# Attention on one core: values loaded in pieces of four keys instead of eight

## The chip, the core and the metric

The kernel runs on one core of a Trainium2 chip. The metric is the device time of one execution in microseconds; lower is better. Five engines work side by side and are kept in step by semaphores: TensorE (PE, with its weight loads as PEld) multiplies matrices, VectorE (DVE) and ScalarE (ACT) read its results, GpSimd (POOL) helps with elementwise work, and SyncE (SP) only issues transfers. The transfers themselves run on 16 DMA engines.

## The reference

```python
B, H, Sq, Sk, D = 16, 32, 192, 1024, 128      # all bf16
def reference(q, k, v):
    scale = q.shape[-1] ** -0.5
    scores = jnp.einsum("bhqd,bhkd->bhqk", q, k) * scale
    p = _softmax(scores, axis=-1)
    return jnp.einsum("bhqk,bhkd->bhqd", p, v)
```

There are 512 heads. Each has 192 queries, 1024 keys and 1024 values of 128 numbers. The order in which the 1024 keys are taken is free, as long as keys and values of a head are taken in the same order.

## The kernel before

**Groups, pairs and units.** Heads are handled in 32 groups of 16 (`G`). Within a group, two heads make a pair, with 384 query rows: three units of 128 rows (A from the first head, B from the second, S with 64 rows of each). Two pairs make one turn of the written-out orders `PE_ORDER`, `DVE_ORDER` and `ACT_ORDER`, in which each engine executes its steps; a tick behind a name means the unit of an earlier turn. A group is four turns, 24 units.

**What happens to a unit.** `qk` multiplies 128 queries by all 1024 keys into PSUM (`s_ps`, two matmuls of 512 columns; four for an S unit). VectorE (L333) copies the scaled scores to SBUF and takes the row extreme. For four of six units ScalarE (L374) takes the exponential, for the other two ("shifted") GpSimd only subtracts (L208) and the exponential comes later. `tr` transposes the 1024 columns in eight blocks of 128 on TensorE (L283, into `pt_ps`), ScalarE moves them to SBUF (L383 or L385), and `pv` multiplies each block `t` by the values of the same 128 keys (L317), summing the eight blocks in `o_ps`. VectorE divides by the row sums and writes bf16 to `ob` (L358). All matmuls are issued in the helper `product`, so the profile gives them its line, L221.

**Which keys make a block.** Keys are loaded with a DMA transpose (L148), so that the 128 numbers of a key lie along the partitions. The source is read as rows of eight keys, `(g p) (t d)` with `t` = 8: key `8 p + t` of a head becomes column `p` of block `t`. The values have to follow: partition `p` gets the eight values `8 p` to `8 p + 7`, which are 2048 consecutive bytes of memory (L138 to L141).

**Who issues what, in which order.** SyncE's queue holds, for each group: the keys of the group two ahead (L148), its queries (L152, also a DMA transpose), and the stores of the group's results (L172) in three parts of 80, 44 and 4 partitions (`STORE_PARTS`). Before the keys it waits until the last `qk` of the group that has used the same buffer (`NS` = 2) is done, before the stores until `ob` is full. The first two groups' values are issued by SyncE too. From then on ScalarE issues a group's values, one DMA of 4 MB, after the step `("ev", 15)` of the group before; it first waits until the buffer's last `pv` is done and until that group's keys have landed (L390 to L394). TensorE waits for the queries and the keys at the first `qk` of a group (L258, L267), and for the values at its first `pv` (L314).

Of the kernel before, what the change touches and what calls it, by code (L numbers as in the profile page):

```python
# [5 lines left out]
BF16 = mybir.dt.bfloat16  # L6
# [27 lines left out]
def _attention_kernel(nc, q, k, v, out, G=16, NS=2, NSS=5, NX=4, NPT=5,  # L34
# [10 lines left out]
    KT_TILES = SK // 128  # L45
# [6 lines left out]
    kf = k.rearrange("b h s d -> (b h) s d")  # L52
    vf = v.rearrange("b h s d -> (b h) s d")
# [16 lines left out]
    with ExitStack() as es:  # L70
        def sb(name, shape, dt):
            return es.enter_context(nc.sbuf_tensor(name, shape, dt))
# [4 lines left out]
        def sem(name):  # L77
            return es.enter_context(nc.semaphore(name))

        kt = sb("kt", [128, NS, KT_TILES, G * 128], BF16)  # L80
        qt = sb("qt", [128, NS, G * SQ], BF16)
        vs = sb("vs", [128, NS, G, KT_TILES, 128], BF16)
        ob = sb("ob", [128, NSO, PPG, 3, 128], BF16)
        ss = sb("ss", [128, NSS, SK], F32)
        nb = sb("nb", [128, NSS], F32)
# [28 lines left out]
        def unit_info(u):  # L114
            name = UNITS[u % 6]
            pr = 2 * (u // 6) + int(name[1])
            return pr, "ABS".index(name[0]), pr // PPG, pr % PPG
# [18 lines left out]
        def load_v(e, g, a, b, sm):  # L136
            h0 = g * G
            e.dma_start(  # L138
                vs[:, g % NS, a:b],
                vf[h0 + a:h0 + b].rearrange("g (p t) d -> p g t d", t=KT_TILES),  # L140
            ).then_inc(sm, 16)  # L141

        @block.sync
        def _(e):
            def load_kq(g, a, b, sems):
                s = g % NS
                h0 = g * G
                e.dma_start_transpose(  # L148
                    kt[:, s, :, a * 128:b * 128],
                    kf[h0 + a:h0 + b].rearrange("g (p t) d -> (g p) (t d)", t=KT_TILES),  # L150
                ).then_inc(sems[0], 16)
                e.dma_start_transpose(  # L152
                    qt[:, s, a * SQ:b * SQ],
                    qf[h0 + a:h0 + b].rearrange("g r d -> (g r) d"),
                ).then_inc(sems[1], 16)

            def loads(g):
                s = g % NS
                last_u = (g - NS + 1) * UPG - 1
                if g >= NS:  # L160
                    e.wait_ge(s_qk, last_u + 1)
                load_kq(g, 0, G, (sxk[s], sxq[s]))
                if g < NS:
                    load_v(e, g, 0, G, svl[s])

            def stores(g, a, b):
                so = g % NSO
                e.wait_ge(s_on, g * PPG + b)
                rows = of[g * G + 2 * a:g * G + 2 * b].rearrange("h r d -> (h r) d").rearrange(
                    "(n p) d -> p n d", p=128)  # L170
                for lo, hi in (((0, 128),) if g == NGR - 1 else STORE_PARTS):
                    e.dma_start(  # L172
                        rows[lo:hi],
                        ob[lo:hi, so, a:b].rearrange("p pg y d -> p (pg y) d"),
                    ).then_inc(sst[so], 16)

            n = len(FIRST)
            for i in range(n):
                load_kq(0, *FIRST[i], (sf[i], sf[i]))
                if i > 0:  # L180
                    for i2 in range(i if i > 1 else 0, i + 1):
                        load_v(e, 0, *FIRST[i2], sfv[i2])
            for g in range(1, min(NS, NGR)):
                loads(g)
            for g in range(NGR):
                if g + NS < NGR:
                    loads(g + NS)
                for a, b in (LAST if g == NGR - 1 else ((0, PPG),)):
                    stores(g, a, b)
            for so in range(min(NSO, NGR)):  # L190
                n = len(range(so, NGR - 1, NSO)) * len(STORE_PARTS)
                if so == (NGR - 1) % NSO:
                    n += len(LAST)
                e.wait_ge(sst[so], 16 * n)
# [23 lines left out]
        def _(pe):  # L218
            def product(o, w, x, at=(0, 0), start=True, stop=True, transpose=False):

                return pe.add_instruction(mybir.InstMatmult(  # L221
                    name=nc.get_next_instruction_name(),
                    engine=mybir.EngineType.PE,
                    ins=[pe.lower_ap(x), pe.lower_ap(w)],
                    outs=[pe.lower_ap(o)],
                    start_tensor_calc=start,
                    stop_tensor_calc=stop,
                    is_transpose=transpose or None,
                    tile_size=(128, w.shape[-1]),
                    tile_position=at,  # L230
                    bass_skip_group_check=True,
                    ldweights=False,
                ))
# [4 lines left out]
            def qk(u):  # L238
                pr, k3, g, pg = unit_info(u)
                s = g % NS  # L240
                a = 2 * pg
                b = 2 * pg + 1
                S = s_ps[u % 2]
                if k3 < 2:
                    x0 = a * SQ if k3 == 0 else b * SQ + 64
                    tiles = [((0, 0), slice(0, 128), a if k3 == 0 else b, qt[:, s, x0:x0 + 128])]
                else:
                    tiles = [
                        ((0, 0), slice(0, 64), a, qt[:, s, a * SQ + 128:a * SQ + 192]),
                        ((0, 64), slice(64, 128), b, qt[:, s, b * SQ:b * SQ + 64]),  # L250
                    ]
                if g == 0:
                    for i, (h, _) in enumerate(FIRST):
                        if h <= b and i not in seen_kq:
                            seen_kq.add(i)
                            pe.wait_ge(sf[i], 32)
                elif u % UPG == 0:
                    pe.wait_ge(sxq[s], load_cnt(g))  # L258
                ins = None
                for c in range(2):  # L260
                    cs = slice(4 * c, 4 * c + 4)
                    for at, ps_, x, w in tiles:
                        if c == 0:
                            pe.ldweights(w, tile_position=at)  # L264
                            if at[1] == 0:
                                if g > 0 and u % UPG == 0:
                                    pe.wait_ge(sxk[s], load_cnt(g))  # L267
                                if u >= 2:
                                    pe.wait_ge(s_max, u - 1)
                        ins = product(S[ps_, cs], w, kt[:, s, cs, x * 128:x * 128 + 128], at)  # L270
                ins.then_inc(s_qk, 1)

            def tr(u):
# [12 lines left out]
            def pv(u):  # L286
                pr, k3, g, pg = unit_info(u)
                s = g % NS
                O = o_ps[pr % 2]
                PTS = pt_sb[:, u % NPT]  # L290
                sl = O_SLOT[k3]
                a = 2 * pg
                b = 2 * pg + 1
                ins = None
                with_rs = shifted(u)
                if k3 < 2:
                    tiles = [((0, 0), slice(0, 128), a if k3 == 0 else b)]
                else:
                    tiles = [((0, 0), slice(0, 64), a), ((0, 64), slice(64, 128), b)]
                pe.wait_ge(s_ev, u + 1)  # L300
                for t in range(KT_TILES):
                    first = t == 0
                    last = t == KT_TILES - 1
                    for at, rows, x in tiles:
                        w = PTS[:, t, rows]
                        pe.ldweights(w, tile_position=at)  # L306
                        if first and at[1] == 0:
                            if g == 0:
                                for i, (h, _) in enumerate(FIRST):
                                    if h <= b and i not in seen_v:  # L310
                                        seen_v.add(i)
                                        pe.wait_ge(sfv[i], 16)
                            elif u % UPG == 0:
                                pe.wait_ge(svl[s], load_cnt(g))  # L314
                            if k3 == 0 and pr >= 2:
                                pe.wait_ge(s_on, pr - 1)
                        ins = product(O[rows, sl, :], w, vs[:, s, x, t, :], at, first, last)  # L317
                        if with_rs:
                            ins = product(O[rows, 3, sl: sl + 1], w, ones[:, 0:1], at, False, last)
                ins.then_inc(s_pv, 1)  # L320
# [112 lines left out]
```

## Time and profile before

| what | value |
|---|---|
| time, median of 3 runs | 1200.33 us (1194.54 to 1207.98) |
| the profiled execution's own time | 1195.41 us |
| its span, first to last instruction | 1193.6 us |
| granted TensorE clock | 0.984 |
| HBM read and written | 134.22 MB and 25.17 MB |
| value load of a group (ScalarE's queue), issue to landing, median | 16.3 us |
| key load (SyncE), issue to landing, median | 21.1 us |
| query load (SyncE), issue to landing, median | 8.4 us |

The profile is one execution. Its page gives, in order: the busy time of each engine; the span in 40 slices; the DMA queues with their packets and the time that these took; the chain of work that ended last, followed back from the end; the costliest groups of instructions; and the DMA issues. Queue q1 is SyncE's, q10 is ScalarE's. SPq and ACTq are the issuing queues of SyncE and ScalarE: a DMA instruction there lasts until its queue has taken it, not until the data has landed. In tables of stretches, each row has the stretch, its length, busy time of PE, PEld, DVE, ACT and POOL with the number of instructions, the granted clock, the mean busy share of the 16 DMA engines (over 1 where the times of packets overlap) and what they moved in GB/s.

### The profile page before, as it was taken

Reading aid. Unit: us, or ns where it says so; the run is one execution under the profiler, and the core shown is the slowest. Engines: PE = TensorE matmul, PEld = TensorE weight load, DVE = VectorE, ACT = ScalarE, POOL = GpSimd, SP = SyncE. Lnnn points to the kernel's source line nnn. Section 1 sums busy time; section 2 is a strip of 40 time slices with the busy share of each in tenths; the row PEclk is TensorE's granted clock in tenths of the full one; section 3 lists DMA queues with packets and bytes.
Section 4 is the critical chain, followed back from the end, with each engine's and each line's share of the span. In section 5 each row is a group of like instructions: output and inputs, shape, how many; then the busy total and the mean of one; then the engine's idle time right before and its main releaser. Section 6 shows DMA issues by size and latency. Waiting matters only on the chain.

```text
span 1193.6 us, 38884 instructions
## 1 busy us (share of the span) xinstructions
PE 1127.5 (94%) x18432; PEld 847.8 (71%) x15360; DVE 1088.2 (91%) x2304; ACT 1082.4 (91%) x1793; POOL 485.8 (41%) x262
## 2 busy tenths in 40 slices
PE   5698999999989999999999999999999999999998
PEld 2476767777767777777776777777777777777766
DVE  5587989999989999999998999999999999999987
ACT  4677989999999999999997999999999999999988
POOL 2233434434434434444443444444344344444432
PEclk9888999999999999999998999999999999999999
DMA  9999999999999999999999999999999999999991
GB/s 234 243 282 268 270 248 247 288 297 290 288 256 267 275 304 281 285 276 274 289 283 280 266 251 279 295 303 278 275 265 268 292 284 290 271 271 277 291 245 41
DMA packets 790348, 321.26 MB, mean 269 GB/s; under 512 B 724641, under 2 KB 724641, under 8 KB 790177
## 3 DMA queue, kind: packets, MB, share of 16 engines
q1 hardware_dynamic: 728257, 192.95, 83.9%
q10 hardware_dynamic: 61920, 125.83, 28.9%
q8 instruction: 132, 2.16, 0.7%
q14 instruction: 39, 0.32, 0.1%
HBM read 134.22 MB, written 25.17 MB: 134 GB/s over the span
## 4 chain that ended last, share of the span: by engine, by line
PE 58%; DMA 29%; ACT 7%; SPq 5%; issue 0%; DVE 0%
PE o_ps L221 21%; PE pt_ps L221 19%; DMA vs<-in_v_dram 19%; PE s_ps L221 18%; DMA qt<-in_q_dram 11%; SPq L148 5%; ACT x_sb L374 4%; ACT pt_sb L385 2%; ACT pt_sb L383 1%; SPq L152 0%; SPq L138 0%; DVE ob L358 0%; DVE rinv L356 0%
## 5 line engine op out<-in xcount | busy, mean ns | idle before, releaser
L333 DVE TENSOR_SCALAR_CACHE_REDUCE ss<-s_ps 128x1024 f32<-128x1024 f32 x768 | 920.4, 1220 | 89.1 <-PE s_ps L221 72.8
L208 POOL TENSOR_TENSOR x_sb<-ss,nb 128x1024 bf16<-128x1024 f32 x256 | 485.1, 1895 | 695.9 <-DVE ss L333 665.7
L374 ACT ACTIVATE x_sb<-ss,nb 128x1024 bf16<-128x1024 f32 x512 | 585.4, 1145 | 12.9 <-DVE ss L333 12.9
L306 PEld LDWEIGHTS <-pt_sb 128*128 128x128 bf16 (+1 forms) x8192 | 443.2, 104 | 213.5 <-issue 115.6
L221 PE MATMUL s_ps<-kt,qt 128*128 128x512 bf16 (+1 forms) x2048 | 467.9, 386 | 47.5 <-DMA qt<-in_q_dram 47.0
L221 PE MATMUL o_ps<-vs,pt_sb 128*128 128x128 bf16 (+1 forms) x8192 | 497.5, 219 | 14.2 <-DMA vs<-in_v_dram 13.9
L221 PE MATMUL pt_ps<-ident,x_sb 128*128 128x128 bf16 x6144 | 453.1, 220 | 1.3 <-ACT pt_sb L383 1.3
L280 PEld LDWEIGHTS <-x_sb 128*128 128x128 bf16 x6144 | 367.5, 98 | 62.5 <-issue 62.1
L385 ACT ACTIVATE pt_sb<-pt_ps 128x512 f32<-128x512 f32 x512 | 306.2, 598 | 78.7 <-PE pt_ps L221 77.8
L383 ACT ACTIVATE pt_sb<-pt_ps 128x1024 bf16<-128x1024 bf16 x256 | 260.4, 1017 | 14.4 <-PE pt_ps L221 14.3
L221 PE MATMUL o_ps<-ones,pt_sb 128*128 128x1 bf16 x2048 | 191.2, 166 | 0.0
L358 DVE TENSOR_TENSOR ob<-o_ps,rinv 128x384 bf16<-128x384 f32 x256 | 142.7, 557 | 8.8
L264 PEld LDWEIGHTS <-qt 128*128 128x128 bf16 (+1 forms) x1024 | 79.6, 104 | 66.6 <-DMA qt<-in_q_dram 44.0
L374 ACT ACTIVATION_READ_ACCUMULATOR x_sb<-ss,nb 128x1 f32 x512 | 100.7, 197 | 0.0
L333 DVE DVE_READ_ACCUMULATOR ss<-s_ps 128x1 f32 x768 | 63.8, 83 | 0.0
L356 DVE RECIPROCAL rinv<-o_ps 128x1 f32<-128x1 f32 x256 | 41.8, 163 | 4.2 <-PE o_ps L221 4.2
L346 DVE RECIPROCAL rinv<-rs 128x2 f32<-128x2 f32 x256 | 40.9, 160 | 1.1 <-ACT x_sb L374 1.1
L374 ACT ACT_TABLE_LOAD x1 | 1.3, 1283 | 0.8 <-PEq L418 0.8
L200 POOL TENSOR_SCALAR_AFFINE_SELECT ident<-ones 128x128 bf16<-128x128 bf16 x1 | 0.3, 295 | 0.1
L198 POOL MEMSET ones<- 128x128 bf16 x1 | 0.2, 205 | 0.3 <-POOLq L418 0.3
L418 POOL MEMSET const-float32-0.0<- 128x1 f32 x1 | 0.1, 100 | 0.3 <-issue 0.3
L418 POOL MEMSET const-uint8-127<- 128x1 uint8 x1 | 0.1, 103 | 0.0
(2 smaller groups left out, 0.2 us busy)
## 6 DMA issues: line engine op xcount, KB each, us to landing
vs<-in_v_dram ACTq DMA_DIRECT2D x30, 4096.0 KB, 16.3
out_dram<-ob SPq DMA_DIRECT2D x31, 480.0 KB
out_dram<-ob SPq DMA_DIRECT2D x31, 264.0 KB
vs<-in_v_dram SPq DMA_DIRECT2D x1, 4096.0 KB, 15.1
vs<-in_v_dram SPq DMA_DIRECT2D x1, 2048.0 KB, 9.9
vs<-in_v_dram SPq DMA_DIRECT2D x1, 1536.0 KB, 8.6
out_dram<-ob SPq DMA_DIRECT2D x31, 24.0 KB
kt<-in_k_dram SPq DMA_TRANSPOSE x34, 21.1
```

The source lines that it names most:

```text
L148: e.dma_start_transpose(kt[:, s, :, a * 128:b * 128], kf[h0 + a:h0 + b].rearrange("g (p t) d -> (g p) (t d)", t=KT_TILES),).then_inc(sems[ ...
L208: gp.tensor_tensor(x_sb[:, u % NX, :], ss[:, u % NSS, :], nb[:, u % NSS: u % NSS + 1].to_broadcast([128, SK]), ALU.subtract,).then_inc(s_x ...
L221: return pe.add_instruction(mybir.InstMatmult(name=nc.get_next_instruction_name(), engine=mybir.EngineType.PE, ins=[pe.lower_ap(x), pe.low ...
L264: pe.ldweights(w, tile_position=at)
L280: pe.ldweights(w, is_transpose=True, tile_position=(0, 0))
L306: pe.ldweights(w, tile_position=at)
L333: dve.tensor_scalar(ss[:, u % NSS, :], s_ps[u % 2][:].rearrange("p t k -> p (t k)"), -scale, None, ALU.mult, ALU.min, accum_out=nb[:, u % ...
L356: dve.reciprocal(rinv[:, pr % 2, sel], o_ps[pr % 2][:, 3, sel]).then_inc(s_ri, 1)
L358: dve.tensor_tensor(ob[:, so, pg], o_ps[pr % 2][:, 0:3, :], rinv[:, pr % 2, 0:3].unsqueeze(2).to_broadcast([128, 3, 128]), ALU.mult,).then ...
L374: act.activation(x_sb[:, u % NX, :], ss[:, u % NSS, :], ACT_FN.Exp, bias=nb[:, u % NSS: u % NSS + 1], scale=-1.0, accum_out=rs[:, pr % NRS ...
L383: act.activation(pt_sb[:, u % NPT], pt_ps[u % 2][:], ACT_FN.Exp, scale=-1.0).then_inc(s_ev, 1)
L385: act.activation(words(pt_sb[:, u % NPT]), words(pt_ps[u % 2][:]), ACT_FN.Copy).then_inc(s_ev, 1)
```

## The change

A head's 1024 keys are taken as two halves (`y`) of 512, and a partition gets four consecutive values of each half: key `512 y + 4 p + t`. One DMA still brings a group's values; each of its contiguous pieces has 1024 bytes. The keys are read as rows of four keys, 256 rows a head, so that a transposed block `t` has 256 columns, the first 128 of half 0 and the others of half 1. A score matmul takes two blocks of 256 columns instead of four of 128. In `pv`, step `t` of eight multiplies by half `t % 2`, key `t // 2` of four. Sizes of buffers, waits and orders stay.

```diff
-        kt = sb("kt", [128, NS, KT_TILES, G * 128], BF16)
+        kt = sb("kt", [128, NS, 4, G * 256], BF16)
-        vs = sb("vs", [128, NS, G, KT_TILES, 128], BF16)
+        vs = sb("vs", [128, NS, 2 * G, 4, 128], BF16)
...
         def load_v(e, g, a, b, sm):
             h0 = g * G
             e.dma_start(
-                vs[:, g % NS, a:b],
-                vf[h0 + a:h0 + b].rearrange("g (p t) d -> p g t d", t=KT_TILES),
+                vs[:, g % NS, 2 * a:2 * b],
+                vf[h0 + a:h0 + b].rearrange("g (y p t) d -> p (g y) t d", y=2, t=4),
             ).then_inc(sm, 16)
...
                 e.dma_start_transpose(
-                    kt[:, s, :, a * 128:b * 128],
-                    kf[h0 + a:h0 + b].rearrange("g (p t) d -> (g p) (t d)", t=KT_TILES),
+                    kt[:, s, :, a * 256:b * 256],
+                    kf[h0 + a:h0 + b].rearrange("g (p t) d -> (g p) (t d)", t=4),
                 ).then_inc(sems[0], 16)
...
-                        ins = product(S[ps_, cs], w, kt[:, s, cs, x * 128:x * 128 + 128], at)
+                        ins = product(S[ps_, cs], w, kt[:, s, 2 * c:2 * c + 2, x * 256:x * 256 + 256], at)
...
-                        ins = product(O[rows, sl, :], w, vs[:, s, x, t, :], at, first, last)
+                        ins = product(O[rows, sl, :], w, vs[:, s, 2 * x + t % 2, t // 2, :], at, first, last)
```

## The prediction, as it was put on record before the changed kernel ran

> **What bounds the kernel now.** I read the page first (parts 1 to 4), then the waits, the chain in order of time, SyncE's own queue, and at last short stretches of the DMA engines.
>
> ```profile
> span 1193.6 us, 38884 instructions
> PE 1127.5 (94%) x18432; PEld 847.8 (71%) x15360; DVE 1088.2 (91%) x2304; ACT 1082.4 (91%) x1793; POOL 485.8 (41%) x262
> DMA  9999999999999999999999999999999999999991
> q1 hardware_dynamic: 728257, 192.95, 83.9%
> q10 hardware_dynamic: 61920, 125.83, 28.9%
> PE 58%; DMA 29%; ACT 7%; SPq 5%; issue 0%; DVE 0%
> ```
>
> Three compute engines stand at 91 to 94% and the DMA engines are never idle. Queue 10 is the value loads issued by ScalarE: 125.83 MB in 61,920 packets, 2 KB each. Queue 1 is everything from SyncE: k, q and the stores, almost all 256 B packets. The chain that ended last is 29% DMA, so transfers do set the time. Which ones, the chain in order of time and the waits tell:
>
> ```profile
> 203.52 1.00 PE pt_ps L221 x16
> 212.15 1.00 PE pt_ps L221 x16
> ...
> 595.25 10.47 DMA qt<-in_q_dram
> ...
> 781.83 16.56 DMA vs<-in_v_dram
> ```
>
> ```profile
> PE s_ps L221 <- DMA qt<-in_q_dram: 47.0, 20, 10.4
> PE o_ps L221 <- DMA vs<-in_v_dram: 13.9, 11, 3.7
> ```
>
> One turn of TensorE's order (four heads) takes 8.63 us where nothing is late (203.52 to 212.15), so a group of 16 heads needs 34.5 us and 32 groups 1105 us. The rest of the span is start, end, and two transfers that are late by a little in turn. (The columns are the total in us, the number of waits and the longest.) The chain has 15 pieces of q and 14 of v: in about half of the groups q landed last, in the other half v. A delay of either shows almost in full in its own half.
>
> SyncE's queue shows why q comes when it does (start, duration):
>
> ```profile
> 129.72 3.50 SPq L172 DMA_DIRECT2D out_dram<-ob  x3
> ...
> 595.25 4.71 SPq L152 DMA_TRANSPOSE qt<-in_q_dram  x1
> 600.00 13.92 SPq L172 DMA_DIRECT2D out_dram<-ob  x3
> 613.97 19.05 SPq L148 DMA_TRANSPOSE kt<-in_k_dram  x1
> ```
>
> k, q, stores, k follow without a gap. The same three stores take 3.50 us to hand over at 129.72, where no values run beside them, and 13.92 us at 600.00, just after ScalarE issued values at 599.43. So the stores wait for their turn among the value packets. In numbers:
>
> ```profile
> 582.00:587.00 5.00, 5.00 (x92) 3.90 (x84) 4.83 (x11) 4.64 (x9) 2.14 (x2) 1.00 1.28 290
> 602.00:604.00 2.00, 2.00 (x50) 1.53 (x45) 1.93 (x6) 2.00 (x4) 1.90 (x1) 1.00 1.03 383
> 606.00:613.00 7.00, 7.00 (x126) 5.51 (x103) 6.25 (x13) 5.45 (x9) 2.65 (x2) 1.00 1.07 380
> 616.00:618.00 2.00, 2.00 (x32) 1.36 (x20) 1.89 (x7) 2.00 (x4) 1.45 (x1) 1.00 0.97 173
> ```
>
> The last column is GB/s. k alone: 290, that is 16 x 256 B / 290 = 14.1 ns a packet on one engine. Values alone: 383, 16 x 2048 / 383 = 85.6 ns a packet. Values beside stores: 380; if one store packet goes for each value packet, a round is 16 x 2304 / 380 = 97.0 ns, and a store packet adds 11.4 ns. When the values are done and k is only starting (616 to 618), 173.
>
> **The change, part by part.** TensorE, VectorE, ScalarE and GpSimd execute the same instructions in the same order. The scores' moving operand is two runs of 256 columns where it was four of 128, still 512 columns, and PV reads the same 128 contiguous columns from another place. I cost both at nothing.
>
> *k in rows of 1024 B.* A group is still one DMA of 16,384 packets of 256 B; they come from rows half as long. The nearest rows are k now (rows of 2 KB: 290 GB/s at 582) and q (rows of 256 B). A stretch with q's packets at 564 to 566 also moves 290 GB/s. A row length between the two that give the same rate I cost at 0; bounds 0 on both sides.
>
> *Values in 1024 B pieces.* A group's 4 MB become 4096 packets instead of 2048, 256 an engine instead of 128. This size is not in the trace. A line through 256 B (14.1 ns) and 2048 B (85.6 ns) gives 44.7 ns for 1024 B: 89.4 for two, +3.8 ns a 2 KB. Where another queue also has packets, v pays one foreign packet for each of its own: (44.7 + 11.4) x 2 = 112.2 against 97.0, +15.2 ns. How much is contested: of the 13.9 us of data at 601.4 to 615.3, the first 2.6 are alone, 2.6 us / 85.6 ns = 30 packets an engine; 98 are contested. So v lands 30 x 3.8 + 98 x 15.2 = 1.6 us later. Lower bound: no price by turns, 128 x 3.8 ns = 0.5 us, or none at all if a 1024 B packet costs exactly half. Upper bound: the page's mean packet times, 0.289 x 16 x 1193.6 us / 61,920 = 89.1 ns (2032 B) and 0.839 x 16 x 1193.6 / 728,257 = 22.0 ns (265 B), whose line gives 50.8 ns for 1024 B, +11.9 ns a 2 KB; 128 x 11.9 + 98 x 11.4 = 2.6 us. I take 1.6, because the mean times hold overlap (k's share of 1.28 says so) and the rates do not.
>
> What hides it? In a q group the values have some slack:
>
> ```profile
> 616.42 0.22 PE L221 MATMUL o_ps<-vs,pt_sb 128*128 128x128 bf16 x1
> ```
>
> They were issued at 599.43 and landed 16.5 us later, at 615.9: slack 0.5 us. In another such group (issue 888.7, landing 16.4 us, first use 906.30) it is 1.2. Mean 0.85, so 1.6 leaves a stall of 0.75 us there. Behind the waiting PV on TensorE stand the transposes and the scores of the next units, so VectorE and ScalarE follow it.
>
> *The other side: SyncE is released sooner.* Stores are passed one for each value packet, and value packets come faster: 13.92 = 0.6 + 13.3 us becomes 0.6 + 13.3 x 56.1 / 97.0 = 8.3 us, so k is issued 5.6 us earlier, at 608.4 in this group. What it waits for, the last score product of the group before, was done by 605.8, when TensorE began the next group's scores, so no wait takes the place of this one. Little of the 5.6 us arrives. The engines were busy, and k's packets stand behind the stores and take turns with the rest of v. What k can win is the hole at 616 to 618: 2 us x (1 - 173/290) = 0.8 us. What it loses is the dearer values: 128 x 3.8 ns = 0.5 us. Net -0.3 us on q's landing. Outer bounds: -0.8 (values free) and +1.5 (128 x 11.9 ns).
>
> *Sum.* 14 v groups x 1.6 = +22.4. 15 q groups x 0.75 = 11.3, of which I count half, +5.6: where the next group is again a q group, its wait for q shrinks by as much. 15 q groups x -0.3 = -4.5. Together +23.5 us on the profiled execution's own time of 1195.4 (span 1193.6): 1218.9. That execution is 4.9 us under the median of the runs shown, 1200.33, so on that scale 1223.8, I say 1224.
>
> **The rivals.**
>
> *A. Faster: values land when they did, and k comes early.* If the engines take turns by bytes, or 1024 B costs half of 2048 B, v keeps its 16.3 us and SyncE's earlier k fills the hole. Then q waits shrink: 29 to 31 groups x 0.8 = about -24 us, within the 47.0 us there are: 1176. For it: stores hold SyncE for 13.92 us. Against it: 380 GB/s beside stores is hardly under the 383 alone, so small packets are not free there. The Trainium skill (DMA: Bandwidth & Descriptors, Specifications) gives 512 B as the least size for line rate, and by that 1024 B would cost nothing extra: it stands on this side, and the sum by it alone would be this rival's 1176. No row here has a 1024 B packet to decide it.
>
> *B. No change.* k's early start wins the whole 0.8 us in q groups and v's lateness is near 0.5 us: 14 x 0.5 - 15 x 0.5 = about 0: 1200. For it: slack of 0.5 to 1.2 us would swallow 0.5. Against it: needs turns to be free and the hole to be filled.
>
> *C. Much slower: values meet k instead of the stores.* At 129.72 the stores were over before v was issued (132.71 in the chain), SyncE issued k at 137.17, and v took 18.75 us to land; the three such groups have the longest v pieces in the chain, 19.71, 18.75 and 17.60 us, a mean of 18.7 against 16.3. With shorter stores the kernel may stay in that order. Then v is late by 18.7 - 16.3 + 1.6 = 4.0 us in each group. Against the present 1 us or so of waiting a group this is +3 x 29 = +87, less the q waits that vanish behind it (47.0 x 0.5): +64, 1264. It decides if SyncE is done with its stores more than some 3 us before v is issued. Against it: the kernel left this order by itself: from 208 us on, stores on SyncE's queue take 14 us beside the values.
>
> **How the numbers follow.** Forecast (v late by about 1.6 us, partly repaid): 0.45, own range 1206 to 1245. A: 0.25. B: 0.15. C: 0.15. The time is the forecast's, 1224. The range reaches into A and to C's value: 1180 to 1268. The runs shown spread from 1194.54 to 1207.98, so a difference under 1% can hardly be told from none. Faster by over 1%: A, 0.25. Within 1%: B, 0.15; the low end of the forecast's own range falls inside it about as often as B's upper end falls outside. Slower by over 1%: 0.45 + 0.15 = 0.60.
>
> **What would show it.** Right: queue 10 has about 123,000 packets and a share above 28.9%; values land in about 18 us; PE's wait for v grows from 13.9 to 35 us or more; the wait for q falls; stores on SyncE take about 8 us and k follows at once; k issue grows by what of v is left. k alone still moves 290 GB/s. Wrong: v's landing stays at 16.3 us (A or B), k alone has another rate (then the k part was mis-costed), or the stores take 3.5 us throughout and v lands in over 19 us (C).

## The result, and the profile after

The changed kernel takes 1290.89 us (median of 4 runs, 1287.86 to 1297.32) where the kernel before takes 1197.43 us (4 runs, 1189.12 to 1207.98): a ratio of 1.0813, interval 1.073 to 1.0895. It is 8% slower. The forecast was slower too, but 1224 us, and the range ended at 1268. Executions over 1.5% above the fastest of their kernel are left out of every ratio and of the medians in the experiments below. The profiled execution has a span of 1286.1 us. Lines of the page and of the waits that answer to those of before:

```profile
span 1286.1 us, 38884 instructions
PE 1156.7 (90%) x18432; PEld 870.1 (68%) x15360; DVE 1089.5 (85%) x2304; ACT 1083.4 (84%) x1793; POOL 485.8 (38%) x262
q1 hardware_dynamic: 732353, 192.95, 80.7%
q10 hardware_dynamic: 123360, 125.83, 32.0%
DMA 45%; PE 35%; ACT 15%; SPq 4%; issue 0%; DVE 0%
...
vs<-in_v_dram ACTq DMA_DIRECT2D x30, 4096.0 KB, 19.1
...
kt<-in_k_dram SPq DMA_TRANSPOSE x34, 30.4
...
PE o_ps L222 <- DMA vs<-in_v_dram: 97.5, 30, 7.9
...
PE s_ps L222 <- DMA qt<-in_q_dram: 25.4, 4, 10.1
```

Queue 10 has 123,360 packets of 1 KB, the DMA share of the chain went from 29 to 45%, and values land 19.1 us after their issue instead of 16.3. TensorE now waits for them 30 times, in 29 of the 30 groups whose values ScalarE issues, 97.5 us in total. For q it waits four times, all in the first 60 us.

The lines add up. Against before, the waits for values grew by 97.5 - 13.9 = 83.6 us, those for q shrank by 47.0 - 25.4 = 21.6, and TensorE's busy time grew by 1156.7 - 1127.5 = 29.2 with the same 18,432 matmuls: 91.2 us in sum, of 92.5 that the span grew. The 29.2 us were in no term of the prediction. Where they come from shows in stretches of one group (columns as before; the last three numbers are the granted clock, the DMA share and GB/s):

```profile
580.00:582.00 2.00, 2.00 (x29) 1.33 (x18) 2.00 (x5) 2.00 (x4) 0.00 (x0) 1.00 1.25 363
582.00:584.00 2.00, 0.04 (x1) 0.00 (x0) 1.88 (x5) 2.00 (x5) 1.90 (x1) 1.00 1.10 279
584.00:586.00 2.00, 0.00 (x0) 0.00 (x0) 0.00 (x0) 0.18 (x2) 0.00 (x0) 1.00 1.22 108
586.00:588.00 2.00, 0.16 (x3) 0.10 (x1) 0.00 (x0) 0.00 (x0) 0.00 (x0) 0.72 1.26 231
588.00:590.00 2.00, 2.00 (x25) 1.76 (x16) 0.00 (x0) 0.04 (x1) 0.00 (x0) 0.50 1.27 290
590.00:592.00 2.00, 2.00 (x16) 1.58 (x15) 1.19 (x2) 0.98 (x1) 0.00 (x0) 0.50 1.28 290
592.00:594.00 2.00, 2.00 (x18) 1.34 (x16) 0.67 (x3) 0.60 (x1) 0.00 (x0) 0.57 1.27 290
594.00:596.00 2.00, 2.00 (x49) 1.47 (x42) 1.62 (x4) 1.50 (x2) 1.31 (x1) 1.00 1.27 290
...
628.00:630.00 2.00, 2.00 (x16) 1.33 (x14) 0.30 (x1) 1.02 (x1) 0.00 (x0) 0.50 1.27 290
```

TensorE stands still from 582 to 587.84, waiting for the values. After that the granted clock is 0.50 for some 6 us, TensorE is busy all the time, and gets through 16 to 25 matmuls in 2 us instead of some 30 to 50. Over the span the granted clock fell from 0.984 to 0.952. The Trainium skill (TensorE: Matmul & The Clock Gate, What's actually happening) has the clock fall to half after an idle window of about 3.4 us; this trace agrees, with 0.50 after a wait of 5.8 us. But shorter waits are followed by half the clock here too: the last row comes after one of 1.9 us, in the next group. So a wait is paid for a second time, in part: over the whole kernel the 83.6 us of added waits bring 29.2 us of added busy time with them.

SyncE's queue and the chain, in the same part of the span:

```profile
565.96 21.84 DMA vs<-in_v_dram
...
609.19 17.92 DMA vs<-in_v_dram
```

```profile
564.87 6.21 SPq L173 DMA_DIRECT2D out_dram<-ob  x3
571.50 28.45 SPq L149 DMA_TRANSPOSE kt<-in_k_dram  x1
600.00 3.32 SPq L153 DMA_TRANSPOSE qt<-in_q_dram  x1
603.36 4.55 SPq L173 DMA_DIRECT2D out_dram<-ob  x3
613.65 25.57 SPq L149 DMA_TRANSPOSE kt<-in_k_dram  x1
...
SPq L149 <- PE s_ps L222: 886.2, 30, 33.1
```

The same wait in the kernel before:

```profile
SPq L148 <- PE s_ps L221: 563.2, 30, 31.4
```

In the group at 600 the stores take 4.55 us to hand over where they took 13.92. SyncE then waits for the score products of the group before and issues the keys at once when the buffer is free, 4.5 us after the values (609.19 to 613.65); its wait for that buffer is 886.2 us where it was 563.2. In the kernel before, keys were issued 14.5 us after the values (599.43 to 613.97). So values and keys now run side by side, the keys' issue lasts 25.57 us instead of 17 to 19, and the landing of the values swings between 16.5 and 24 us from group to group.

This is rival C of the prediction in its early keys, but not in what makes the values late. C had them late where they meet the keys instead of the stores. The two groups shown differ the other way. At 609.19 the stores had been handed over 1.3 us before the values were issued, the keys came 4.5 us after the values, and these landed in 17.92 us. At 565.96 the stores had been issued 1.1 us before the values and were still being handed over (until 571.08), the keys came at 571.50, and the values landed in 21.84 us. The whole trace divides like this. In ten groups the stores were handed over 0.9 to 2.0 us before the values were issued: 16.5 to 18.1 us. In eight they were issued 0.3 to 2.5 us before the values and still being handed over, with the keys behind them within 6 us: 20.3 to 24.0 us. The latest values are those that meet the stores and then the keys.

### The profile page after: what moved, and what is told of

It is laid out like the page before. It is cut to its first block, busy times and chain, and to the rows that moved or that the text cites. A ratio compares the mean times of both kernels' runs of the same rounds, so it can differ in the third digit from the quotient of the medians.

```text
span 1286.1 us, 38884 instructions
## 1 busy us (share of the span) xinstructions
PE 1156.7 (90%) x18432; PEld 870.1 (68%) x15360; DVE 1089.5 (85%) x2304; ACT 1083.4 (84%) x1793; POOL 485.8 (38%) x262
## 3 DMA queue, kind: packets, MB, share of 16 engines
q10 hardware_dynamic: 123360, 125.83, 32.0%
## 4 chain that ended last, share of the span: by engine, by line
DMA 45%; PE 35%; ACT 15%; SPq 4%; issue 0%; DVE 0%
DMA vs<-in_v_dram 45%; PE o_ps L222 13%; PE pt_ps L222 12%; PE s_ps L222 10%; ACT x_sb L375 9%; ACT pt_sb L386 4%; SPq L149 4%; ACT pt_sb L384 2%; SPq L153 1%; SPq L139 0%; DVE ob L359 0%; DVE rinv L357 0%
## 5 line engine op out<-in xcount | busy, mean ns | idle before, releaser
L307 PEld LDWEIGHTS <-pt_sb 128*128 128x128 bf16 (+1 forms) x8192 | 455.2, 105 | 307.3 <-issue 211.3
L222 PE MATMUL o_ps<-vs,pt_sb 128*128 128x128 bf16 (+1 forms) x8192 | 510.3, 221 | 98.7 <-DMA vs<-in_v_dram 97.5
L222 PE MATMUL s_ps<-kt,qt 128*128 128x512 bf16 (+1 forms) x2048 | 476.3, 391 | 26.0 <-DMA qt<-in_q_dram 25.4
L222 PE MATMUL pt_ps<-ident,x_sb 128*128 128x128 bf16 x6144 | 462.7, 223 | 1.6 <-ACT pt_sb L384 1.6
L281 PEld LDWEIGHTS <-x_sb 128*128 128x128 bf16 x6144 | 377.5, 100 | 62.1 <-issue 61.7
L222 PE MATMUL o_ps<-ones,pt_sb 128*128 128x1 bf16 x2048 | 194.9, 168 | 0.0
L265 PEld LDWEIGHTS <-qt 128*128 128x128 bf16 (+1 forms) x1024 | 80.8, 105 | 43.3 <-DMA qt<-in_q_dram 20.8
## 6 DMA issues: line engine op xcount, KB each, us to landing
vs<-in_v_dram ACTq DMA_DIRECT2D x30, 4096.0 KB, 19.1
```

Of the source, the lines that this page charges most:

```text
L222: return pe.add_instruction(mybir.InstMatmult(name=nc.get_next_instruction_name(), engine=mybir.EngineType.PE, ins=[pe.lower_ap(x), pe.low ...
L281: pe.ldweights(w, is_transpose=True, tile_position=(0, 0))
```

## The experiments

Each time is a median; each ratio is against runs of the kernel before on the same chip, with its interval.

**Which half of the change?** `k4_only` changes the keys alone:

```diff
-        kt = sb("kt", [128, NS, KT_TILES, G * 128], BF16)
+        kt = sb("kt", [128, NS, 4, G * 256], BF16)
...
-                    kt[:, s, :, a * 128:b * 128],
-                    kf[h0 + a:h0 + b].rearrange("g (p t) d -> (g p) (t d)", t=KT_TILES),
+                    kt[:, s, :, a * 256:b * 256],
+                    kf[h0 + a:h0 + b].rearrange("g (p t) d -> (g p) (t d)", t=4),
...
-                        ins = product(S[ps_, cs], w, kt[:, s, cs, x * 128:x * 128 + 128], at)
+                        ins = product(S[ps_, cs], w, kt[:, s, :, x * 256 + c:x * 256 + 256:2], at)
```

> Only the keys are read in rows of four; the values stay in 2048 B pieces (a score matmul reads every second column of a block, so that the order of keys fits). Theory P (price of the value packets) and theory O (order: the stores no longer hold SyncE up, so the next keys are issued early and meet the values): as before, 1197 us within 1%, value landing 16.3 us. Rival K (the shorter key rows cost): about 1290 us, with k alone under 290 GB/s.

1192.02 us, ratio 1.0032 (0.9984 to 1.008). Keys land in 21.0 us (21.1 before), values in 16.2. `v1k_only` changes the values alone, and loads them in two DMAs of 2 MB a group instead of one of 4 MB:

```diff
-        vs = sb("vs", [128, NS, G, KT_TILES, 128], BF16)
+        vs = sb("vs", [128, NS, 2, G, 4, 128], BF16)
...
-            e.dma_start(
-                vs[:, g % NS, a:b],
-                vf[h0 + a:h0 + b].rearrange("g (p t) d -> p g t d", t=KT_TILES),
-            ).then_inc(sm, 16)
+            for y in range(2):
+                e.dma_start(
+                    vs[:, g % NS, y, a:b].rearrange("p g t d -> p g (t d)"),
+                    vf[h0 + a:h0 + b].rearrange("g (p y t) d -> y p g (t d)", y=2, t=4)[y],
+                ).then_inc(sm, 16)
...
-                        ins = product(O[rows, sl, :], w, vs[:, s, x, t, :], at, first, last)
+                        ins = product(O[rows, sl, :], w, vs[:, s, t // 4, x, t % 4, :], at, first, last)
```

> Only the values are loaded in 1024 B pieces (two DMAs of 2 MB a group, one for each half of a partition's eight keys); the keys stay in rows of eight. P and O: 1270 to 1310 us, value landing near 19 us, k issue lasting about 26 us instead of 17.7. K: 1197 us within 1%.

1291.35 us, ratio 1.0857 (1.0764 to 1.0951). The whole loss comes with the 1024 B pieces of the values; the shorter key rows show no cost (0.8% at the end of the interval).

**Is it their price, or the order?** `after_late5` and `before_late5` hold the keys back, in the changed kernel and in the one before:

```diff
-                    e.wait_ge(s_qk, last_u + 1)
+                    e.wait_ge(s_qk, last_u + 1 + 5)
```

> The changed kernel, but SyncE waits for five more score units before it issues a group's keys, about 6.6 us later in a group than now: where the kernel before issued them. O: the values meet the stores and not the keys, landing back to about 17.9 us, wait of TensorE for values from 97 to 40-60 us, 1215 to 1235 us. P (the values are late by their own packets, whoever they meet): no gain, 1280 us or more.

> The kernel before with the same later key issue. O: its steady state has this order already, so little changes there; the first four groups, in which values met keys, lose their stalls: 1185 to 1200 us. P: the same as before, 1197 us. If the later issue itself costs, it shows here as more wait for q.

1232.01 us (1.0371, 1.0276 to 1.0466) and 1186.85 us (0.9975, 0.9938 to 1.0011). So the later keys take 53 to 59 us from the changed kernel (by the ratios and by the medians) and at most a little from the other. Lines of `after_late5`:

```profile
PE 1141.6 (93%) x18432; PEld 857.4 (70%) x15360; DVE 1089.4 (88%) x2304; ACT 1082.9 (88%) x1793; POOL 485.3 (39%) x262
...
vs<-in_v_dram ACTq DMA_DIRECT2D x30, 4096.0 KB, 18.0
...
PE o_ps L222 <- DMA vs<-in_v_dram: 61.0, 29, 4.1
PE s_ps L222 <- DMA qt<-in_q_dram: 24.6, 6, 9.0
```

The same sum against before gives 47.1 - 22.4 + 14.1 = 38.8 us; its span of 1232.5 is 38.9 over that of before. With the keys held back in both kernels, values land at 18.0 against 16.2 us, 1.8 us apart, and the times are 45 us apart. That is about the price of the packets. The order isn't quite the same in the two: by their timelines the keys come 11.8 us after the values here, and 14.5 us after them in `before_late5` (medians). The other half of the loss belongs to the order.

**Are the last 45 us the values' own lateness?** Then an earlier issue of the values should take it back. `after_late3_v13` and `before_late3_v13`:

```diff
-VALUES_AFTER=("ev", 15)
+VALUES_AFTER=("ev", 13)
...
-                    e.wait_ge(s_qk, last_u + 1)
+                    e.wait_ge(s_qk, last_u + 1 + 3)
```

> The changed kernel with the keys issued three score units later and the values two ScalarE steps earlier, after (ev, 13). If what is left after the order is mended is the values' own lateness of about 1.8 us a group, the earlier issue (about 2.5 us) takes most of it: 1195 to 1215 us, wait for values under 25 us. If earlier values only meet more of the stores or ScalarE then waits for the keys: 1230 us or more.

> The same two edits on the kernel before. Its values are hardly late (7.5 us of wait in all with the keys five units later), and its values are issued when the keys have landed, not by the step: little to win, 1180 to 1200 us. If ScalarE is held by the earlier wait for the keys: over 1200 us.

1213.57 us (1.0156, 1.0097 to 1.0214) and 1187.01 us (0.9956, 0.9924 to 0.9988). In the first, values still land in 18.0 us, but the wait for them is down from 61.0 to 9.7 us with a longest of 1.7, and the granted clock is 0.993. Its lines:

```profile
PE o_ps L222 <- DMA vs<-in_v_dram: 9.7, 10, 1.7
PE pt_ps L222 <- ACT pt_sb L386: 30.4, 23, 2.9
PE pt_ps L222 <- ACT pt_sb L384: 16.6, 31, 1.0
```

So an earlier issue takes most of the wait back, but only some of the 45 us: the two spans are still 27.8 us apart (1212.9 and 1185.1). Of these, 9.7 us are waits for values, which `before_late3_v13` doesn't have, and 16.1 are waits for ScalarE's copies to SBUF, 47.0 against 30.9 us. What makes ScalarE later was not tested; it waits for the keys before it issues the values, and the keys take 25.3 us to land here and 21.0 there. `before_late3_v13` beats the kernel before, by half a per cent.

**Is it enough that keys are issued early?** `before_store1` and `after_store1` store a group in one DMA, `after_even3` in three of 48, 48 and 32 partitions:

```diff
-STORE_PARTS=((0, 80), (80, 124), (124, 128))
+STORE_PARTS=((0, 128),)                      # store1
+STORE_PARTS=((0, 48), (48, 96), (96, 128))   # even3
```

> The kernel before, with a group's results stored in one DMA instead of three, so that SyncE hands them over at once and issues the next keys as soon as their buffer is free; values stay in 2048 B pieces. Theory O (values meet keys because SyncE is no longer held): slow with large pieces too, 1240 to 1290 us, k issue lasting 24 to 28 us as in the first groups of before, value landing 18 to 19 us. Theory P (only the size of the pieces): 1190 to 1205 us.

> The changed kernel with one store DMA a group, which all 16 engines share evenly: 192 store packets an engine where the three DMAs give 120 to 240. SyncE is released at once. Theory S (shield: on SyncE's ring the keys' packets stand behind the stores', one store packet goes for each value packet, and values meet keys only where the stores run out first): about 200 contested value packets meet 192 store packets nearly everywhere, landing 17.5 to 18.5 us, 1215 to 1245 us. Theory R (keys issued early are enough to hurt): 1280 us or more.

> The changed kernel with three store DMAs of 48, 48 and 32 partitions, evenly on 16 engines, so that SyncE is held for a while as well. S: 1210 to 1240 us. R: a little under after, 1260 to 1290 us.

`before_store1`: 1200.72 us (1.0058, 1.0011 to 1.0104), against theory O. Its SyncE is released at once:

```profile
568.57 0.61 SPq L172 DMA_DIRECT2D out_dram<-ob  x1
572.16 27.16 SPq L148 DMA_TRANSPOSE kt<-in_k_dram  x1
...
574.00:581.00 7.00, 6.88 (x116) 5.31 (x96) 5.97 (x13) 5.88 (x11) 2.35 (x2) 1.00 1.06 381
```

Keys are issued 3.6 us after the stores, and yet values land in 16.3 us in the median: at 574 to 581 the engines move 381 GB/s, the rate of values with stores (380 before), not that of keys (290). The keys' packets stand behind the stores' in SyncE's queue. So early keys alone do not make 2 KB values late. But some groups are late, the one at 422.13 the most:

```profile
421.34 0.58 SPq L172 DMA_DIRECT2D out_dram<-ob  x1
426.60 27.54 SPq L148 DMA_TRANSPOSE kt<-in_k_dram  x1
...
422.13 20.80 DMA vs<-in_v_dram
...
PE o_ps L221 <- DMA vs<-in_v_dram: 34.3, 17, 4.8
```

In 11 of the 30 groups the values land in 17.6 to 20.8 us, and TensorE's wait for values is 34.3 us where it was 13.9. In all eleven the stores had been handed over 0.2 to 2.4 us before the values were issued. In the 15 groups whose values were issued before the stores were handed over, they land in 15.8 to 16.5 us. So the order has its price with large pieces as well: values issued shortly behind the stores are late.

From this run I formed theory S. It was wrong in size: `after_store1` took 1264.72 us (1.0649, 1.0605 to 1.0694) and `after_even3` 1277.61 us (1.0774, 1.0711 to 1.0837), above what S allowed, with values landing in 18.7 and 19.6 us.

**Without stores.** `before_nostores` and `after_nostores`:

```diff
             def stores(g, a, b):
+                if g < NGR - 1:
+                    return
...
```

> The changed kernel without the stores of all groups but the last (their results are left out). Values still meet keys, but no stores. If meeting keys alone is what hurts: landing stays at 19 us and the time above 1260 us. If what hurts is that the values meet the stores and then also the keys, so many foreign packets in sum: landing 16.5 to 17.5 us as in those groups of after where the stores were over, 1200 to 1235 us.

> The kernel before without the stores of all groups but the last (their results are left out): no shield at all, pieces of 2048 B. Values meet keys after some 6 us, with about 50 packets an engine left. By the packet prices it is 50 x 15.2 + 78 x 3.8 ns = 1.1 us a group quicker than the changed kernel without stores (1212 us): 1175 to 1190 us. If large pieces meeting keys were as bad as in the first groups of before: 1220 us or more.

1212.05 us (1.016, 1.0111 to 1.0208) for the changed kernel, 1164.26 us (0.9808, 0.9742 to 0.9874) for the one before: by the ratios some 42 us apart, with values landing at 17.6 and 16.5 us. So, by the ratios again, the stores cost the kernel before some 23 us and the changed one 78. Values that meet keys alone pay about the price of the packets and no more; it takes stores and keys one after the other to make the landing 19 us and more.

**Turns or standstills?** In the group above the engines move only 108 GB/s at 584 to 586. Keys alone have such standstills in the kernel before, and values with stores alone have none in 10 us:

```profile
588.00:590.00 2.00, 2.00 (x39) 1.65 (x26) 1.93 (x4) 2.00 (x5) 0.90 (x1) 1.00 1.23 75
604.00:614.00 10.00, 8.57 (x145) 6.36 (x118) 8.38 (x19) 8.45 (x15) 3.65 (x2) 1.00 1.06 368
```

To tell whether they delay the values, keys were loaded by plain DMAs:

```diff
+                    e.dma_start(                                                   # kplain
+                        kt[:, s].rearrange("p t (n d) -> p (t n) d", d=128),
+                        kf[h0:h0 + G].rearrange("g (t p) d -> p (g t) d", p=128),
+                    ).then_inc(sems[0], 16)
...
+                    rows = kf[h0:h0 + G].rearrange("g (p t) d -> t p g d", t=8)    # kplain256
+                    flat = kt[:, s].rearrange("p t (n d) -> p (t n) d", d=128)
+                    for t in range(8):
+                        e.dma_start(flat[:, G * t:G * t + G], rows[t]).then_inc(sems[0], 16)
...
```

> The changed kernel, the keys of all groups but the first loaded by a plain DMA in 16,384 pieces of 256 B, as many and as large as the transposing DMA moves; the keys are then not transposed, so the scores are others. Theory X (values beside keys suffer from standstills of the DMA engines that come with the transpose): values land in about 17 us, no stretches under 150 GB/s while both run, 1195 to 1235 us. Theory T (key packets take turns, transposed or not): landing 19 us, 1270 us or more.

> The same plain key load in the kernel before, as the yardstick. X: the keys lose their own standstills of 2 x 1.4 us a group, and the wait for q (47 us) shrinks: 1150 to 1185 us. T: 1190 to 1200 us. The distance of the two plain-key kernels is then what the packet size of the values costs without standstills: 30 to 50 us.

1410.7 us (1.1824, 1.1663 to 1.1985) and 1234.54 us (1.0351, 1.0267 to 1.0435). These did not test what they should: the page of `before_kplain` shows 126,976 packets between 512 B and 2 KB where there were 0, so the key pieces went as 1024 B packets. Values landed in 22.9 us beside them, and in 16.1 in the kernel before, which keeps them apart. Beside these keys the values are later still; that the size of the foreign packets does it was not tested apart. With pieces that lie apart:

> The changed kernel, keys of all groups but the first loaded by eight plain DMAs a group in 256 B pieces whose neighbours lie 256 KB apart; not transposed, so the scores are others. Theory X (standstills that come with the transpose): values land in 17 to 18 us although keys are issued early, no stretch of 2 us under 250 GB/s while both run, 1200 to 1240 us. Theory T (turns of key packets of this number and size): landing 19 us or more, 1270 us or more.

> The yardstick, the same key load in the kernel before: if plain 256 B packets go as fast as transposed ones (290 GB/s), 1165 to 1200 us with values landing in 16 us. If they are slower, the wait for q grows and the kernel with it; then only the landing of the values in the two can be compared.

1225.28 us (1.0276, 1.0225 to 1.0328) and 1226.93 us (1.0289, 1.0245 to 1.0333), landing 17.7 and 16.2 us. Here SyncE was kept busy by eight key DMAs a group and did not get ahead: it waited 30.7 us for score products instead of 886.2. So the values met mostly stores, and the pair gives the price of the packets once more, 1.5 us, but not the answer. The 1.5 us cost no time here: in `before_kplain256` TensorE waits 78.4 us for q and 0.5 for values, in `after_kplain256` 53.4 and 30.8. A better test leaves out the stores as well:

> The changed kernel without the stores of all groups but the last (their results are left out) and with the keys of all groups but the first loaded plainly in 256 B pieces (not transposed, so the scores are others); beside after_nostores (1212 us, landing 17.6 us, stretches at 156 and 228 GB/s while values and keys both run). Theory X (standstills of the transpose): landing 15.3 to 16.3 us, no such stretches, 1165 to 1195 us. Theory T (turns of key packets, transposed or not): landing 17.3 us or more, 1200 us or more.

1225.22 us (1.0313, 1.0221 to 1.0405):

```profile
vs<-in_v_dram ACTq DMA_DIRECT2D x30, 4096.0 KB, 17.8
...
PE o_ps L231 <- DMA vs<-in_v_dram: 55.9, 30, 3.6
```

17.8 us, beside 17.6 with transposed keys: theory X missed its 15.3 to 16.3. Stretches with values and keys side by side, first of `after_nostores_kplain`, then of `after_nostores`:

```profile
584.00:586.00 2.00, 2.00 (x42) 1.65 (x24) 1.92 (x6) 2.00 (x5) 0.50 (x1) 1.00 1.08 368
590.00:592.00 2.00, 2.00 (x47) 1.53 (x39) 1.97 (x5) 2.00 (x4) 1.73 (x1) 1.00 1.12 312
592.00:594.00 2.00, 2.00 (x31) 1.37 (x19) 2.00 (x5) 2.00 (x5) 0.00 (x0) 1.00 1.19 294
594.00:596.00 2.00, 0.17 (x1) 0.00 (x0) 1.89 (x7) 2.00 (x4) 1.87 (x1) 1.00 1.21 213
```

```profile
541.00:543.00 2.00, 2.00 (x29) 1.41 (x24) 1.97 (x5) 2.00 (x4) 1.04 (x1) 1.00 1.18 228
545.00:547.00 2.00, 2.00 (x36) 1.32 (x28) 1.97 (x5) 2.00 (x5) 1.39 (x1) 1.00 1.14 364
```

With plain keys there is no drop to 228 GB/s while the bulk of the values moves; the 213 from 594 on is beside their tail, which lands at 596.3. But the rate beside the values sinks to about 300, where transposed keys have 364 between their drops. So values beside keys are late without the transpose too. How the lateness beside transposed keys divides into turns and standstills is not settled, because plain keys lower the rate by themselves.

**Two more.** `before_even3_late3_v13` puts `even3` and `late3_v13` together in the kernel before; `v512_late5` takes the change one step further (values in four quarters of two keys, keys in rows of two, late keys).

> A version of the kernel before with all three edits that helped or should: stores evenly on 16 engines, keys three score units later, values two steps earlier. Even stores end sooner on the lower engines: 1170 to 1188 us. If only the order counted, which the late keys already set: as without even stores, 1187 us.

> The changed kernel with the late keys, but one step further: values in pieces of 512 B (two keys, four quarters of a head, keys in rows of two). By the line of packet prices 512 B takes 24.3 ns. If the values give a turn away for each of their packets while stores run: 98 x (4 x 35.7 - 97.0) + 30 x (4 x 24.3 - 85.6) ns = 4.8 us a group later than in pieces of 2048 B, landing 20.5 to 21.5 us, 1310 to 1345 us. If it is only the packet's own overhead: 128 x 11.6 ns = 1.5 us, 1225 to 1245 us. If the store packets run out (they are fewer than the value packets): in between.

The first: 1198.51 us (1.0101, 1.0039 to 1.0164), slower than 1187.01 without the even stores; the split into 80, 44 and 4 partitions is better. The second: 1328.35 us (1.114, 1.0986 to 1.1294). The time is in the expected range, but for no reason that was expected: the page shows 61,920 packets for the values, no more than with 2 KB pieces, and they landed in 19.9 us, not 20.5 or later. It is inconclusive for the price of turns. It does show that the number of packets is not all that shorter pieces cost: with half the packets of `after_late5` and the same hold on the keys, the values landed 1.9 us later. The price of the packets in this document is that of the 1024 B pieces, as they were loaded here.

## Why the prediction was wrong

**Right.** Key rows of 1024 B cost 0: `k4_only`. The price of a packet came out of the two sizes as worked out: at 620 to 623, values beside keys, the engines move

```profile
620.00:623.00 3.00, 3.00 (x62) 2.19 (x56) 2.93 (x8) 2.76 (x5) 1.90 (x1) 1.00 1.13 363
```

or 16 x 1280 / 363 = 56.4 ns for a value packet and a foreign one, if they go in turns, where the prediction had 44.7 + 11.4 = 56.1. Values land 1.6 us later by their own packets: measured 1.8 us (`after_late5` against `before_late5`) and 1.5 us (the `kplain256` pair), each with nearly the same order in both kernels. The direction was right, and q stops being the wait. Rivals A and B fell with the landing: in no version of the changed kernel did the median come under 17.6 us.

**The step that failed first: "Little of the 5.6 us arrives".** I let SyncE's earlier release end in -0.3 us on q, as though keys behind stores and beside values only shared the same work in another order. It is a question of who is late. Values that meet the stores and then the keys land in 20.3 to 24.0 us, the median of all is 19.1, and TensorE stands still until they are there. Taking the early keys away gave 53 to 59 us back. The stores' hand-over was also misjudged. Where it runs wholly beside values it takes 9.5 and 9.8 us (at 805.85 and 1116.80), not 8.3; in about half of the groups it is over before the values are issued, and takes 3.5 to 4.7 us.

**The second: 14 v groups and 15 q groups.** The sum charged 1.6 us to 14 groups and half of 0.75 to 15. With values late everywhere there are no q groups left: TensorE waits for values in 29 of 30 groups, and 29 times even with late keys. 29 x 1.6 = 46 us is close to the 45 that `after_late5` lost to `before_late5`, but the closeness is partly luck: the waits for values grew by 53.5 us and the busy time by 15.7, and the waits for q shrank by 19.8. The slack of 0.5 to 1.2 us was that of groups that had waited for q, and goes with that wait.

**A term that was missing: the clock.** In the trace of the changed kernel each of the 15 waits for values of 3.4 to 8.0 us, and four of the nine of 1.5 to 2.8 us, is followed by half the granted clock for 3.4 or 6.8 us, and the busy time grows by 29.2 us. Where the longest wait for values is 1.7 us (`after_late3_v13`), the clock is 0.993.

**The rivals.** C, with 0.15, saw the early keys coming and priced them at 1264, without the clock and with half the waits for q taken off. Its condition, stores over more than some 3 us before the values are issued, holds in no group: the longest lead is 2.0 us, and the groups with a lead of 0.9 us and more are the quick ones. So C was right about the keys and wrong about the stores, and its 3 us of added waiting in each group is near the measured 83.6 / 29 = 2.9 partly by luck. Its argument against itself, that the kernel had left that order on its own, holds only while values are no later than the budget of some 16 us between their issue and first use. 1.6 us more is over it in every group: late values delay TensorE, TensorE delays the next values' issue, and the stores get ahead. That chain was argued from the trace, not tested by itself. What stays open, beside the share of the standstills, is how the two halves of the order, stores and keys, add up to 19 us: theory S, one turn of a store for a turn of a value until the stores run out, gave too small a loss by 20 to 40 us.

## What to carry to other kernels

Where a transfer lands just in time, halving its pieces does not cost the packets' price alone: find what stands beside it on other queues, and what that is held back by. A queue that looks blocked (stores that take 14 us to hand over) may be what keeps two large transfers apart. Before believing a lateness of a microsecond or two, look at whether the waiting engine's clock survives it.

## What had not been expected of the hardware

Two plain loads whose 256 B and 512 B pieces are neighbours in memory across neighbouring partitions show as packets of 1024 and 2048 B, four pieces in one (126,976 and 61,920 packets). And keys alone stand still at times: 75 GB/s in a stretch of 2 us between stretches at 290 GB/s. Plain keys beside values had no such drop while the bulk of the values moved, but a lower rate (294 to 312 GB/s against 364), and were no kinder to the values (17.8 us against 17.6).
